# One raw weight piece requested ahead from step 16 on, and the rows' scatter released behind a finish: windowed attention with a mixture of experts on one core

## The chip, the cores and the metric

The kernel runs on one core of a Trainium2 chip, in one launch. The metric is the device time of an execution in microseconds. In what follows PE is TensorE, DVE is VectorE, ACT is ScalarE, POOL is GpSimd and SP is SyncE, which here only issues transfers.

## The reference

Attention over 8 batches of 8 heads, 576 positions, head width 64, with a causal window of 64. Its rows (4608 tokens of 512 values) go through a mixture of eight experts, each token through its best expert alone.

```python
scores = scale * np.matmul(q, k.transpose(0, 1, 3, 2))
mask = (rel >= 0) & (rel < window)                 # rel = i - j, window = 64
scores = np.where(mask, scores, -1000000000.0)
...
out_attn = np.matmul(attn, v)                      # softmax of scores, times v
x = out_attn.transpose(0, 2, 1, 3).reshape(B * S, H * D)
...
logits = x @ w_gate + modality_bias[modality_id]   # (4608, 8)
e_idx = np.argmax(logits, axis=1)
...
for e in range(E):
    h = np.maximum(x[mask] @ w1[e], 0.0)           # 512 -> 1024
    out[mask] = gate_w[mask, None] * (h @ w2[e])   # 1024 -> 512
```

## The kernel before

**Steps.** The attention is cut into 36 pairs of 64-row blocks, one pair of 128 tokens a step. The loop over `s` is a software pipeline written out by hand: in step `s` the scores of pair `s` are computed, the probabilities of pair `s-1` are turned, the values and the attention rows `xa` of pair `s-2` are made, and the router's logits of pair `s-3`. Every engine's order is the order in which the code is written (`manual_schedule`), so a line that is moved in the loop moves on each engine past whatever was recorded between its old and its new place.

**Rows.** Two pairs form a group G. `route1` to `route3` rank its tokens by expert; `rows` then turns the ranks into indices (L821, DVE) and POOL scatters the two pairs' rows into the scratch `xs` in DRAM, ordered by expert (L808 and L809). From group 4 on `rows` is not run at once but put into `held`; `release` runs what is left in `routing` (L752 to L765 on DVE) and then the held `rows`, once in each even step from 14 on. There are five `xa` buffers, so the attention rows of pair p+5 are written (L707) where those of pair p have been scattered from.

**Slots.** From step 12 on expert work is laid into the same loop. A slot is up to 256 rows of one expert, read back from `xs` into `xt`; `slot_pieces` is a generator that emits a slot's matmuls in 16 pieces, and `gap` takes the next piece. Steps from 12 on have four gaps each, so a slot spans four steps. What a piece leaves for other engines to do is put into `later`, and `run_later` emits it. `finish` is one such thing: it multiplies a half slot's result (`y0` or `y1`, 128x512 in PSUM) by the gate into an SBUF tile `y` (L334, DVE), and POOL scatters that tile to the output (L337). The first half's last matmuls are the first gap of steps 16, 20, 24, 28, 32 and 36, the second half's the fourth gap of the same steps; the second finish therefore stands on DVE just ahead of the next step's logits (L730) and attention rows (L707).

**Weights.** The weights of two experts are kept in SBUF, 16 pieces of 128x512 f32 each. A raw piece is loaded by SP (L103 or L107) into a tile `y`; a later call of `weights` rounds it into `Whi` (`split_hi`, L114, ACT), the call after that puts the rest into `Wlo` (`split_lo`, L119, DVE). Calls stand at the end of every step from 5 on, three a step in steps 12 to 15, and from step 16 on also in the middle of odd steps. The pieces 1 to 20 are requested by the end of step 15, the last at the end of step 23 or 24.

**The shared buffers.** Raw pieces and finished tiles both come from one pool, `y` with `bufs=4`. A new tile takes the buffer whose last use was emitted longest ago, and the writer waits until that use is over: for a finished tile until its scatter has landed.

Of the kernel before, what the change touches and what calls it, by code (L numbers as in the profile page):

```python
# [26 lines left out]
def tile_window_attn_moe(  # L27
# [39 lines left out]
    FIRST = 12  # L67
# [31 lines left out]
    def load_piece(raw, ev, c):  # L99

        if c * WCH < WC:
            ch, f0 = divmod(c * WCH, F)
            nc.sync.dma_start(  # L103
                out=raw, in_=w1_v[bass.ds(ev, 1), :, ch, f0:f0 + WCH].rearrange("o p f -> (o p) f"))
        else:
            c2 = c - WC // WCH
            nc.sync.dma_start(out=raw, in_=w2_v[bass.ds(ev, 1), :, c2, :].rearrange("o p f -> (o p) f"))  # L107
        return raw

    def split_hi(raw, buf, c):  # L110

        if Whi[buf] is None:
            Whi[buf] = wpool.tile([P, 2 * WC], F32R, name="Whi1")
        nc.scalar.copy(out=Whi[buf][:, c * WCH:(c + 1) * WCH], in_=raw)  # L114

    def split_lo(raw, buf, c):

        cols = slice(c * WCH, (c + 1) * WCH)
        nc.vector.tensor_tensor(  # L119
            out=Wlo[buf][:, cols], in0=raw, in1=Whi[buf][:, cols].bitcast(F32), op=ALU.subtract)  # L120
# [8 lines left out]
    def tick(n=1, table=False):  # L129
        for _ in range(n):  # L130
            if routing and not table:
                routing.pop(0)()
            elif queue:
                queue.pop(0)()
                issued[0] += 1
# [111 lines left out]
    def run_later():  # L247
        while later:
            later.pop(0)()
# [265 lines left out]
    def turn_bank(s):  # L515

        i = n_tp[0]
        n_tp[0] += 1
        if s < FIRST and i % 5 > 1:
            return ps_m.tile([P, 512], F32, name=("em", "y0", "y1")[i % 5 - 2])  # L520
        return ps_t.tile([P, 512], F32, name="tp")
# [31 lines left out]
    def quartered(G):  # L553

        return G >= QUARTERS and GBLK * G // BPB == (GBLK * G + GBLK - 1) // BPB
# [9 lines left out]
    def turn_heads(G, nm, i):  # L565

        dst = by_group(qT if nm == "q" else kT)[:, G % 2, 2 * i:2 * i + 2]
        nc.vector.transpose(
            out=dst.rearrange("p h j i -> p (h j i)"),
            in_=by_heads(qk[G, nm]).rearrange("p h u d -> p (h u d)"))  # L570
# [23 lines left out]
    def heads_t(G, nm, i, tp):  # L594


        src = plain(qk[G, nm], HP if quartered(G) else H).rearrange("p t (h a) d -> p t h (a d)", a=2)
        for h in range(2):
            for t in range(2):
                n = 2 * h + t  # L600
                turn(tp[:, n * P:(n + 1) * P], src[:, t, 2 * i + h])

    def heads_out(tp, G, nm, i, copy):
        dst = by_group(qT if nm == "q" else kT)[:, G % 2, 2 * i:2 * i + 2]
        copy(out=dst.rearrange("p h j (i t) -> p h t (j i)", t=2),
             in_=tp.rearrange("p (h t i) -> p h t i", h=2, t=2))
# [130 lines left out]
    def release():  # L737

        if held:
            tick(len(routing))  # L740
            held.pop(0)()
# [28 lines left out]
    def route2(G, tp):  # L770

        while routing:
            routing.pop(0)()
        oh = chosen[G]
        rk = tp[:, 0:GB * E]
        nc.tensor.matmul(
            out=rk, lhsT=tri, rhs=oh[:, 1:].rearrange("p j e -> p (j e)"), start=True, stop=False)
        for j in range(GB):
            sh = [P, GB - j, E]
            nc.tensor.matmul(  # L780
                out=rk[:, j * E:], lhsT=ones, rhs=oh[:, j:j + 1, :].broadcast_to(sh),
                start=False, stop=(j == GB - 1))
        return rk
# [117 lines left out]
    pieces = []  # L901
    raws = []
# [144 lines left out]
    def weights(s):  # L1047

        if halves:
            split_lo(*halves.pop(0))  # L1050
        if len(raws) == 2 or raws and not pieces:
            split_hi(*raws[0])
            halves.append(raws.pop(0))
        while pieces and len(raws) < 2:
            x, c = pieces.pop(0)
            raw = epool.tile([P, WCH], F32, name="y", bufs=4)
            raws.append((load_piece(raw, evs[x], c), x, c))

    for s in range(NPR + 4):
        j = s % GB  # L1060
        if s <= FIRST:
            for f, args in at.pop(s, ()):
                f(*args)
        n_tick = 6 if s < FIRST else 5
        n_gap = 0 if s < FIRST else 4
        G = s // GB + 1
        heads = PARTS[j] if G < NG else ()
        R = (s - 5) // GB if s >= 5 and j == 1 else -1

        def part(i):  # L1070
            if not heads:
                return
            if i == 1 and quartered(G):
                turn_heads(G, *heads[1])
                return
            tp = turn_bank(s)
            heads_t(G, *heads[i], tp)
            heads_out(tp, G, *heads[i], nc.scalar.copy if heads[i] == K1 else nc.vector.tensor_copy)

        def ranks():  # L1080
            if R < 0:
                return None
            tp = turn_bank(s)
            rk = route2(R, tp)
            n = None
            if R == NG - 1 or any(R == T for T, _ in EARLY):
                n = counts_out(tab if R == NG - 1 else pl, counts(R, tp))
            route3(R, rk)
            return n
        if 1 <= s < FIRST:  # L1090
            swap_upper(s - 1)

        if 2 <= s < NPR + 2:
            values(s - 2)
            if s <= FIRST:
                values_out(s - 2)
        if 3 <= s < NPR + 3:
            logits(s - 3, turn_bank(s) if s != FIRST else ps_m.tile([P, 512], F32, name="y0"))
            if (s - 3) % GB == GB - 1:
                route1((s - 3) // GB)  # L1100
        if FIRST < s < NPR + 2:
            values_out(s - 2)
        if s < NPR:
            scores(s)
            if s == FIRST:
                x_turn(fetched[0])
                gap(it, True)
            minima(s)
            if s == FIRST - 2:
                tick(todo[0][-1] - issued[0], table=True)  # L1110
        if 1 <= s <= NPR:
            if s == FIRST:
                run_later()
            if s >= FIRST:
                swap_upper(s - 1)
            swap_v(s - 1)
            for a in range(2):
                probs_t(s - 1, a, turn_bank(s))
            sums(s - 1)
        if s < NPR:  # L1120
            exps(s, (0, 1))
        if s == 0:
            first_pair(1, (both[:1], both[1:]))
            cast_bias()
        if s <= FIRST:
            if s >= 2:
                x_t(s - 2, turn_bank(s) if s != FIRST else ps_m.tile([P, 512], F32, name="y0"))
            run_later()
            tick(2)
            if s < NPR:  # L1130
                exps(s, (2, 3, 4))
            part(0)
            if s == FIRST:
                weights(s)
                gap(it, True)
            run_later()
            tick(n_tick)
            cnt = ranks()
            exps(s, (5, 6, 7))
        else:  # L1140
            release()
            gap(it, True)
            run_later()
            tick(2)
            if s < NPR:
                exps(s, (2, 3, 4))
            if s < FIRST + 4 or s % 2:
                weights(s)
            for f, args in at.pop(s, ()):
                f(*args)  # L1150
            gap(it, True)
            cnt = ranks()
            if s < NPR + 2:
                x_t(s - 2, turn_bank(s))
            part(0)
            run_later()
            tick(n_tick)
            if s < NPR:
                exps(s, (5, 6, 7))
        if n_gap > 2:  # L1160
            if FIRST <= s < FIRST + 4:
                weights(s)
            gap(it, True)
        part(1)
        run_later()
        tick(n_tick)
        if s == WEIGHTS:
            load_weights()
        if s >= WEIGHTS:
            weights(s)  # L1170
        if n_gap > 3:
            gap(it, True)
        run_later()
        if s == 1:
            select_bias()
        if s == 4:
            nc.sync.dma_start(out=xs_blk[DUMMY:DUMMY + 2].rearrange("b p c -> p b c"), in_=padrow)
        for T, xs_ in EARLY:
            if T == R:
                plan(T, xs_, cnt)  # L1180
# [271 lines left out]
```

## Time and profile before

| what | value |
|---|---|
| median of 3 runs | 629.34 us (627.99 to 630.23) |
| the profiled execution, its own time | 624.07 us |
| span of the profiled execution, first to last instruction | 622.3 us |
| granted TensorE clock, mean | 0.989 of full speed |
| PE busy | 600.2 us (96%) |
| DVE, ACT, POOL busy | 389.3, 293.7, 140.9 us |

Steps 12 to 35 of the attention loop lie between 75.84 and about 330 us, most of them 10.0 to 10.8 us long; behind them only slots are worked off. In a row of instructions in order of time the first number is the start, the second the length, both in us; then engine, line, operation, what it writes and reads, shapes, and in brackets how long the engine was idle before and what ended that. A row of the waits has the total, the number of times and the longest. In a table by stretch each engine has its busy time; PEclk is the granted clock.

### The profile page before, as it was taken

The page shows a single profiled execution, that of the slowest core. Times are in us where ns is not written, and L with a number is a line of the kernel's source. Part 1 is how long each engine was busy: PE and PEld are TensorE (multiplying, and loading weights), DVE is VectorE, ACT ScalarE, POOL GpSimd, SP SyncE. Part 2 cuts the span into 40 slices and gives each one's busy share as a digit, 9 for nine tenths or more (in the row PEclk, how much of TensorE's full clock was granted, in tenths as well). Part 3 has the DMA queues.
Part 4 walks back from the last instruction along what each step waited for, and adds up shares of the span by engine and source line. Part 5 has one row for each costly group of instructions (what it writes and reads, how often), then busy time and mean ns, then how long its engine had stood idle before and what let it go on. Part 6 is the DMA issues. An engine that isn't in the chain of part 4 may idle for free.

```text
span 622.3 us, 17338 instructions
## 1 busy us (share of the span) xinstructions
PE 600.2 (96%) x6309; PEld 537.6 (86%) x6309; DVE 389.3 (63%) x1493; ACT 293.7 (47%) x926; POOL 140.9 (23%) x315
## 2 busy tenths in 40 slices
PE   7999889979999989999999999999999999999996
PEld 5888778868889878988898899899999999989986
DVE  3899988857867776767656365323224734776621
ACT  3899885753756556555553111111112513554411
POOL 6333322132142212320423131011001111102202
PEclk7999999999999999999999999999999999999999
DMA  9998957656757735554513034622243534678300
GB/s 167 219 242 213 223 159 181 158 152 152 171 152 183 197 84 137 154 111 102 148 53 105 35 101 151 188 71 69 44 159 101 171 135 136 190 252 241 114 17 22
DMA packets 175111, 88.08 MB, mean 142 GB/s; under 512 B 138746, under 2 KB 157744, under 8 KB 174896
## 3 DMA queue, kind: packets, MB, share of 16 engines
q1 hardware_dynamic: 166400, 67.46, 44.6%
q0 software_dynamic: 5888, 18.93, 8.1%
q8 instruction: 50, 0.82, 0.5%
q10 hardware_dynamic: 2736, 0.58, 0.5%
q14 instruction: 37, 0.30, 0.2%
HBM read 67.49 MB, written 23.91 MB: 147 GB/s over the span
## 4 chain that ended last, share of the span: by engine, by line
PE 70%; DVE 5%; DMA 5%; SPq 3%; issue 2%; ACT 2%; POOL 1%; POOLq 0%; DVEq 0%; ACTq 0%
PE y L326 27%; PE em L304 19%; PE sp L304 10%; PE tp L470 6%; PE av L696 2%; PE sp L640 2%; DMA out_dram<-y,id 2%; SPq L590 2%; DMA xs_scratch<-xa,idx 1%; PE tp L725 1%; DVE xt L266 1%; PE y L377 1%; DMA xt<-xs_scratch 1%; DVE xl L196 1%; POOL xs_scratch L809 1%
## 5 line engine op out<-in xcount | busy, mean ns | idle before, releaser
L326 PE MATMUL y<-Whi,hh 128*128 128x512 f32 x288 | 116.3, 404 | 0.0
L666 ACT ACTIVATE ss<-ss,mn 128x128 f32<-128x128 f32 x288 | 112.2, 397 | 6.6 <-DVE mn L654 6.6
L326 PE MATMUL y<-Wlo,hh 128*128 128x512 f32 x288 | 113.2, 393 | 0.0
L326 PE MATMUL y<-Whi,hl 128*128 128x512 f32 x288 | 112.9, 392 | 0.0
L313 DVE SCALAR_TENSOR_TENSOR hl<-em,hh 128x512 fp32r<-128x512 f32 x50 | 34.4, 689 | 79.5 <-ACT hh L312 79.1
L337 POOL DMA_INDIRECT out_dram<-y,id x36 | 39.7, 1104 | 191.0 <-DVE y L334 160.8
L304 PE MATMUL em<-xh,Whi 128*128 128x256 f32 x400 | 81.7, 285 | 0.0
L304 PE MATMUL em<-xl,Whi 128*128 128x256 f32 x400 | 79.2, 279 | 0.0
L304 PE MATMUL em<-xh,Wlo 128*128 128x256 f32 x400 | 79.1, 279 | 0.0
L312 ACT ACTIVATE hh<-em 128x512 fp32r<-128x512 f32 x50 | 29.9, 599 | 100.5 <-PE em L304 95.5
L675 ACT COPY pT<-tp 128x512 f32<-128x512 f32 x57 | 31.5, 589 | 83.3 <-PE tp L470 83.0
L809 POOL DMA_INDIRECT xs_scratch<-xa,idx x36 | 36.6, 1017 | 128.9 <-DVE e_n_p L154 58.9
L326 PEld LDWEIGHTS y<-Whi,hl 128*128 128x128 f32 x288 | 54.3, 189 | 12.2
L654 DVE CUSTOM_DVE_ANT_0 ss<-sp,masks 128x128 f32<-128x128 f32 x288 | 63.4, 285 | 2.3 <-PE sp L640 2.3
L304 PEld LDWEIGHTS em<-xh,Whi 128*128 128x128 f32 x400 | 62.8, 188 | 2.3
L326 PEld LDWEIGHTS y<-Whi,hh 128*128 128x128 f32 x288 | 54.7, 190 | 8.9
L326 PEld LDWEIGHTS y<-Wlo,hh 128*128 128x128 f32 x288 | 54.5, 189 | 8.5
L304 PEld LDWEIGHTS em<-xh,Wlo 128*128 128x128 f32 x400 | 60.9, 188 | 0.0
L304 PEld LDWEIGHTS em<-xl,Whi 128*128 128x128 f32 x400 | 60.8, 188 | 0.0
L666 ACT ACTIVATION_READ_ACCUMULATOR ss<-ss,mn 128x1 f32 x288 | 55.9, 194 | 0.0
L312 ACT ACTIVATE hh<-sp 128x512 fp32r<-128x512 f32 x22 | 13.1, 597 | 76.1 <-PE sp L304 76.1
L696 PEld LDWEIGHTS av<-ve,pT 128*64 128x64 f32 x576 | 36.3, 138 | 12.6 <-issue 8.1
(242 smaller groups left out, 1201.7 us busy)
## 6 DMA issues: line engine op xcount, KB each, us to landing
xt<-xs_scratch SPq DMA_DIRECT2D x72, 128.0 KB, 2.9
vo<-in_v_dram SPq DMA_DIRECT2D x32, 256.0 KB, 3.3
y<-in_moe_w_dram SPq DMA_DIRECT2D x32, 256.0 KB, 2.8
vo<-in_moe_w_dram SPq DMA_DIRECT2D x24, 256.0 KB, 3.6
ss<-in_moe_w_dram SPq DMA_DIRECT2D x24, 256.0 KB, 4.2
xs_scratch<-xs_scratch SPq DMA_DIRECT2D x8, 514.0 KB, 5.8
pT<-in_moe_w_dram SPq DMA_DIRECT2D x16, 256.0 KB, 4.5
qk<-in_k_dram SPq DMA_DIRECT2D x22, 128.0 KB, 3.9
```

What stands on the lines that cost most here:

```text
L304: nc.tensor.matmul(out=hb[:, i * TP:(i + 1) * TP], lhsT=w[buf][:, c0:c0 + P], rhs=x[:, c * TP:(c + 1) * TP], start=(n == 0), stop=(n == le ...
L312: nc.scalar.activation(out=hh, in_=hb, func=AF.Relu),
L313: nc.vector.scalar_tensor_tensor(out=hl, in0=hb, scalar=0.0, in1=hh.bitcast(F32), op0=ALU.max, op1=ALU.subtract)))
L326: nc.tensor.matmul(out=sl["y", t], lhsT=h[:, i * TP + t * P:i * TP + (t + 1) * P], rhs=w[buf][:, c0:c0 + DM], start=(k == 0 and n == 0), s ...
L337: ins = nc.gpsimd.indirect_dma_start(out=out, out_offset=bass.IndirectOffsetOnAxis(ap=sl["id"][:, t:t + 1], axis=0), in_=y, in_offset=None ...
L470: nc.tensor.transpose(out=out_, in_=in_, identity=ident[p0:p0 + n, p0:p0 + n])
L590: dma.dma_start(out=by_heads(t)[rows, (h - nh) // 2, u, :], in_=src.rearrange("(u p) d -> p u d", p=R32))
L654: nc.vector.tensor_tensor_reduce(out=ss[a][:, hp, :], in0=sp[a][:, hp * P:(hp + 1) * P], in1=mask, scale=-1.0 / 8.0, scalar=3.0e38, op0=AL ...
L666: nc.scalar.activation(out=ss[a][:, hp, :], in_=ss[a][:, hp, :], func=AF.Exp, bias=mn[:, h:h + 1], scale=-1.0, accum_out=sm[:, h:h + 1])
L675: nc.scalar.copy(out=pT, in_=pp)
L696: nc.tensor.matmul(out=by_block(av)[c * W64:(c + 1) * W64, a, :, hp, :], lhsT=pT[:, i:i + W64], rhs=(vo if c else ve)[p][:, 2 * hp + a, :] ...
L809: ins = nc.gpsimd.indirect_dma_start(out=xs, out_offset=bass.IndirectOffsetOnAxis(ap=idx[:, j:j + 1], axis=0), in_=xg[j], in_offset=None)
```

## The change

Two edits in the loop of steps. From step 16 on `weights` keeps one raw piece requested ahead instead of two: `n` is 1, so the call at the end of step 16 requests nothing, and each later call first converts the one piece at hand and then requests the next. And in steps from 13 on `release` stands behind the first gap and its `run_later` instead of ahead of them.

```diff
         if halves:
             split_lo(*halves.pop(0))
-        if len(raws) == 2 or raws and not pieces:
+        n = 2 if s < FIRST + 4 else 1
+        if len(raws) >= n or raws and not pieces:
             split_hi(*raws[0])
             halves.append(raws.pop(0))
-        while pieces and len(raws) < 2:
+        while pieces and len(raws) < n:
             x, c = pieces.pop(0)
             raw = epool.tile([P, WCH], F32, name="y", bufs=4)
             raws.append((load_piece(raw, evs[x], c), x, c))
...
         else:
-            release()
             gap(it, True)
             run_later()
+            release()
             tick(2)
```

The order of PE and ACT stays as it was. On DVE and POOL it changes in six places, steps 16, 20, 24, 28, 32 and 36, all alike; on SP the loads of the raw pieces 21 to 32 move.

DVE in step 16, ahead of the change: the copy of `ve`, the routing operations that `release` runs (`lm` to `oh`), the indices of the rows (`idx`) and the first finish (`y` from `y_2120`, the slot's `y0`).

```order
L543 COPY ve<-vo 64x512
L752 TENSOR_REDUCE lm<-lg 128x2
L753 TENSOR_TENSOR lg<-lg,lm 128x16
L757 SCALAR_TENSOR_TENSOR wn<-lg,desc 128x16
L759 TENSOR_REDUCE wm<-wn 128x2
L760 TENSOR_TENSOR oh<-wn,wm 128x16
L765 TENSOR_REDUCE oh<-oh 128x8
L821 CAST idx<-dst 128x2
L334 TENSOR_SCALAR y<-y_2120,gate 128x512
L605 COPY kT<-tp 128x2x2x128
```

The same place with the change:

```order
L543 COPY ve<-vo 64x512
L334 TENSOR_SCALAR y<-y_2120,gate 128x512
L752 TENSOR_REDUCE lm<-lg 128x2
L753 TENSOR_TENSOR lg<-lg,lm 128x16
L757 SCALAR_TENSOR_TENSOR wn<-lg,desc 128x16
L759 TENSOR_REDUCE wm<-wn 128x2
L760 TENSOR_TENSOR oh<-wn,wm 128x16
L765 TENSOR_REDUCE oh<-oh 128x8
L821 CAST idx<-dst 128x2
L605 COPY kT<-tp 128x2x2x128
```

The finish moved ahead of the seven routing operations, and these behind it.

POOL in the same step, before: the two row scatters (`xs_scratch`) and the scatters of the two finished tiles, `y_2659` of the first half and `y_2737` of the second.

```order
L808 COPY xa0_101<-idc_210 128x1
L809 DMA xs_scratch<-xa0_101,idx_2496 39168x514
L808 COPY xa1_102<-idc_210 128x1
L809 DMA xs_scratch<-xa1_102,idx_2496 39168x514
L336 MEMSET pause_100 1x1
L337 DMA out_0_dram<-y_2659,id_1854 4608x512
L337 DMA out_0_dram<-y_2737,id_1854 4608x512
```

With the change, where the two finished tiles are called `y_2647` and `y_2735`:

```order
L336 MEMSET pause_100 1x1
L337 DMA out_0_dram<-y_2647,id_1854 4608x512
L808 COPY xa0_101<-idc_210 128x1
L809 DMA xs_scratch<-xa0_101,idx_2496 39168x514
L808 COPY xa1_102<-idc_210 128x1
L809 DMA xs_scratch<-xa1_102,idx_2496 39168x514
L337 DMA out_0_dram<-y_2735,id_1854 4608x512
```

The first half's scatter moved ahead of both row scatters and their small copies; the second half's stays behind them. (A second `pause` ahead of the last row is left out in both.)

SP at the turn from step 16 to 17, before, with the raw pieces 21 and 22 (`y_2729`, `y_2843`) and 23 (`y_2918`):

```order
L590 DMA qk_2670<-in_q_dram 32x8x32 x8
L107 DMA y_2729<-in_moe_w2_dram 128x512
L107 DMA y_2843<-in_moe_w2_dram 128x512
L529 DMA vo_2845<-in_v_dram 128x8x64
L584 DMA qk_2847<-in_k_dram 128x4x64 x2
L590 DMA qk_2847<-in_k_dram 32x8x32 x8
L103 DMA y_2918<-in_moe_w1_dram 128x512
```

With the change (`y_2841` is piece 21, `y_2916` piece 22; address computations between the loads are left out in both):

```order
L590 DMA qk_2670<-in_q_dram 32x8x32 x8
L107 DMA y_2841<-in_moe_w2_dram 128x512
L529 DMA vo_2843<-in_v_dram 128x8x64
L584 DMA qk_2845<-in_k_dram 128x4x64 x2
L590 DMA qk_2845<-in_k_dram 32x8x32 x8
L107 DMA y_2916<-in_moe_w2_dram 128x512
```

One raw load fewer stands ahead of step 17's loads of `v` and `k`; from there on each place in the queue carries the piece that stood one place earlier.

The four `y` buffers, A to D by address, as the two built programs hand them out from step 16 on (first finish, second finish, and the raw piece requested next):

| step of the first finish | before | with the change |
|---|---|---|
| 16 | C, C, then raw in C | C, C, then raw in B |
| 20 | A, D, with a raw in A between them and one in D behind | C, C, with a raw in A between them and one in D behind |
| 24 | B, B | C, C, with a raw in B between them |
| 28 | C, B | A, C |
| 32 | A, D | D, B |
| 36 | C, B | A, C |

## The prediction

> **What bounds the kernel now.** I read the page first, then busy time by stretch, the waits, and the instructions in order of time around the longest wait. The page says that TensorE is nearly always busy and carries most of the chain that ended last:
>
> ```profile
> PE 600.2 (96%) x6309; PEld 537.6 (86%) x6309; DVE 389.3 (63%) x1493; ACT 293.7 (47%) x926; POOL 140.9 (23%) x315
> PE 70%; DVE 5%; DMA 5%; SPq 3%; issue 2%; ACT 2%; POOL 1%; POOLq 0%; DVEq 0%; ACTq 0%
> ```
>
> So an edit off TensorE counts only where TensorE stands still. A table by step finds such places. These rows are steps 17, 21, 25, 29 and 33, each from its first score matmul to that of the next step; the columns are length, busy time by engine, granted clock, DMA share, GB/s.
>
> ```profile
> core 0: us, PE busy (x) PEld busy (x) DVE busy (x) ACT busy (x) POOL busy (x), PEclk, DMA share, GB/s
> 127.89:143.90 16.01, 12.30 (x141) 10.44 (x137) 7.73 (x34) 6.35 (x22) 3.76 (x8) 0.89 0.53 134
> 174.77:185.46 10.69, 10.69 (x144) 9.52 (x141) 7.72 (x34) 6.24 (x22) 3.20 (x6) 1.00 0.62 166
> 216.20:229.12 12.92, 10.99 (x144) 9.50 (x140) 7.80 (x34) 5.85 (x21) 2.88 (x6) 1.00 0.48 120
> 259.93:270.72 10.79, 10.79 (x143) 9.52 (x140) 6.05 (x31) 5.23 (x20) 2.87 (x6) 1.00 0.58 139
> 301.11:311.26 10.15, 10.15 (x140) 9.12 (x136) 6.01 (x30) 5.23 (x20) 2.87 (x6) 1.00 0.49 133
> ```
>
> Steps 21, 29 and 33 are as long as TensorE is busy. Steps 17 and 25 are not: 3.71 and 1.93 us idle, and in step 17 the granted clock falls to 0.89 as well. The waits of VectorE and of the SP queue name what was late:
>
> ```profile
> DVE y L334 <- DMA out_dram<-y,id: 8.1, 2, 5.1
> DVE xa L707 <- DMA xs_scratch<-xa,idx: 0.5, 1, 0.5
> SPq L107 <- DMA out_dram<-y,id: 18.5, 3, 10.4
> ```
>
> Two waits of VectorE, 8.1 us in all, are for an output scatter that must land before its `y` buffer is written again. Here is the longer one, VectorE first, then POOL, then what followed on ACT and PE:
>
> ```profile
> 122.31 0.17 DVE L752 TENSOR_REDUCE lm<-lg 128x2 f32<-128x16 f32 x1
> 123.51 0.75 DVE L334 TENSOR_SCALAR y<-y,gate 128x512 f32<-128x512 f32 x1
> 126.86 0.68 DVE L119 TENSOR_TENSOR Wlo<-y,Whi 128x512 fp32r<-128x512 f32 x1
> 132.68 0.75 DVE L334 TENSOR_SCALAR y<-y,gate 128x512 f32<-128x512 f32 x1 [5.14 <-DMA out_dram<-y,id]
> 133.69 0.69 DVE L707 TENSOR_TENSOR xa<-av,rw 128x512 f32<-128x512 f32 x1
> ...
> 124.39 1.05 POOL L809 DMA_INDIRECT xs_scratch<-xa,idx  x1 [5.74 <-DVE y L334]
> 125.92 0.96 POOL L809 DMA_INDIRECT xs_scratch<-xa,idx  x1 [0.28 <-POOL xa L808]
> 127.19 1.22 POOL L337 DMA_INDIRECT out_dram<-y,id  x1 [0.22 <-DVE hl L313]
> 133.71 0.99 POOL L337 DMA_INDIRECT out_dram<-y,id  x1 [5.25 <-DVE rw L704]
> ...
> 134.69 0.40 ACT L666 ACTIVATE ss<-ss,mn 128x128 f32<-128x128 f32 x1 [3.04 <-DVE mn L654]
> 137.50 1.08 PE L470 MATMUL tp<-ident_r,qk 128*128 128x128 f32 x4 [2.40 <-issue]
> ```
>
> `y0` (the first finish, 123.51) is ready at 124.26, yet POOL issues its scatter at 127.19, behind both scatters of the rows. `y1` (the second finish) takes the same buffer; VectorE was free for it at 127.54 and waits until 132.68. The minima come late, ACT's exponentials behind them, and TensorE waits for a bank.
>
> **The change, part by part.** *The rows' release behind the finish* takes POOL's two row scatters (some 2.8 us, 124.39 to 127.19) and VectorE's seven small routing operations (122.31 to 123.51) from in front of `y0` in steps 16, 20, 24, 28, 32 and 36. In step 16 `y0` then starts at 122.31 and takes 0.75; `y1`'s scatter shows 0.28 from the end of the write (133.43) to the issue (133.71), so `y0`'s issues at 122.31 + 0.75 + 0.28 = 123.34 instead of 127.19. POOL was idle there (5.74). When does it land? The chain gives 5.36 for the old place behind the rows and, for a second row scatter, 4.11; the view of line 337 gives minimum, median and maximum of all output scatters:
>
> ```profile
> 127.19 5.36 DMA out_dram<-y,id
> 150.93 4.11 DMA xs_scratch<-xa,idx
> ...
> DMA to landing us min/median/max: 2.7/4.1/6.8
> ```
>
> So it lands at 126.0, 127.4 or 130.1 against the 127.54 at which `y1` wants the buffer: a wait of 0, 0 or 2.6. The median is the nearest value, since the scatter is alone in front of its queue but beside loads of `q`: no wait. The Trainium skill ("DMA: Bandwidth & Descriptors", section on the anatomy of one DMA, SWDGE path) gives about 2.0 us plus bytes over 436 GB/s for a DMA from GpSimd, an estimate of 2.6 us for this 256 KB; by that it would land at 125.9 and the sum would be the same. The row's minimum is near it, its median is not, so the row is used.
>
> Steps 20/21 and 24/25 go by these rows:
>
> ```profile
> 168.76 0.17 DVE L752 TENSOR_REDUCE lm<-lg 128x2 f32<-128x16 f32 x1
> 174.58 0.75 DVE L334 TENSOR_SCALAR y<-y,gate 128x512 f32<-128x512 f32 x1
> 175.60 0.69 DVE L707 TENSOR_TENSOR xa<-av,rw 128x512 f32<-128x512 f32 x1
> 170.83 1.05 POOL L809 DMA_INDIRECT xs_scratch<-xa,idx  x1 [7.43 <-DVE y L334]
> ...
> 210.18 0.17 DVE L752 TENSOR_REDUCE lm<-lg 128x2 f32<-128x16 f32 x1
> 218.94 0.75 DVE L334 TENSOR_SCALAR y<-y,gate 128x512 f32<-128x512 f32 x1 [2.99 <-DMA out_dram<-y,id]
> ```
>
> In step 24 the same working gives an issue at 211.21 and a median landing at 215.3, before the 215.95 at which VectorE is free: this wait goes too. In step 20 the new allocation makes `y0` and `y1` share a buffer where they did not: issue 169.79, median landing 173.9, needed at 174.58: no wait; with 6.8, 2.0 us.
>
> What the two stalls are worth. Step 17: against step 33, whose `q` heads are turned in the same way, 16.01 − 10.15 = 5.9; by its own row 3.71 idle plus 0.11 × 16.01 = 1.8 of lost clock, 5.5. I take 5.6. Step 25: against the mean of 21 and 29 (10.74) 2.2, by idle 1.9; I take 2.1. Together 7.7, with ends 7.4 and 8.1. Step 25 also shows how much lateness of VectorE is hidden: a wait of 2.99 lengthened the step by 2.18, so 0.8 costs nothing.
>
> The rows pay for it. Their indices come 0.66 later (one `y` write), and the first row scatter moves from 124.39 to about 125.05 (POOL is through with `y0`'s at 124.56 and still copies ids for 0.2). The five `xa` buffers go round, so L707 of the next step waits for just this scatter. All row scatters, minimum, median, maximum:
>
> ```profile
> DMA to landing us min/median/max: 3.1/4.2/6.1
> ```
>
> In step 17 it lands at 128.2, 129.3 or 131.2; without the stall L707 would start 1.01 after `y1`, at 128.55: a wait of 0, 0.7 or 2.6, of which 0.8 is hidden. In step 21 (171.49 + 4.2 = 175.7 against 175.60) it is 0.1. I take nothing, with 1.8 as the end for step 17. In step 36 `y0` now reaches VectorE before its matmuls end:
>
> ```profile
> 332.88 0.17 DVE L752 TENSOR_REDUCE lm<-lg 128x2 f32<-128x16 f32 x1
> 333.20 0.40 PE L326 MATMUL y<-Whi,hl 128*128 128x512 f32 x1
> ```
>
> That is 333.60 − 332.88 = 0.7 us, under the 0.8.
>
> *One raw piece ahead* moves twelve loads (pieces 21 to 32) one call of `weights` later and past the `vo`, `q`, `k` or slot loads of that call on SP; the conversions stay. It also frees SP: the raw load of step 17 gets a buffer that VectorE's subtraction frees, not `y1`'s, so SP's waits for output scatters (18.5 us) mostly go. By itself I give that nothing: step 21 stands behind the 10.4 us wait and is no longer than step 29, which has none. The price is a shorter lead. Shortest is step 19, where the load follows a slot's load:
>
> ```profile
> y<-in_moe_w_dram SPq DMA_DIRECT2D x32, 256.0 KB, 2.8
> ...
> 158.38 0.36 SPq L103 DMA_DIRECT2D y<-in_moe_w_dram  x1
> 161.62 0.61 ACT L114 CAST Whi<-y 128x512 fp32r<-128x512 f32 x1
> 162.56 1.14 ACT L195 CAST xh<-xt 128x512 fp32r<-128x512 f32 x2 [0.32 <-DVE xt L266]
> 165.79 1.26 ACT L675 COPY pT<-tp 128x512 f32<-128x512 f32 x2 [2.10 <-PE tp L470]
> ```
>
> The piece now converted at 161.62 is the one issued at 158.38: 3.24 us for a landing of 2.8. Should it come a microsecond late, 0.32 of it falls into ACT's idle time, the slot's cast (162.56) moves by 0.7, and ACT has caught up before its next copy, which waits 2.10 for TensorE: under the 0.8, so 0 to 0.2 on TensorE. I put 0.2 for all new waits together.
>
> Sum: −5.6 − 2.1 + 0.2 = −7.5 us, from 624.07 to about 616.6 in the profiled execution (span 622.3 to 614.8). The median of the runs, 629.34, lies 5.3 above that execution and nothing in the trace says where; I carry it over unchanged: **621.8 us**. About 0.3%, 1.9 us, is what a measurement of this kernel can tell from no change.
>
> **The rivals.** *Only part of the stall goes:* `y0`'s scatter, now next to SP's unblocked loads, lands as late as the slowest row. With 6.8 us the waits at steps 17, 21 and 25 are 2.6, 2.0 and 2.1, less 0.8 hidden each, 4.3 in all: 626.1. With the 5.36 of the old place only 0.4 is left at step 17: 622.2. For it: both share the 16 DMA engines, 48% to 62% busy in the table by step. Against: 5.36 was measured behind two row scatters.
>
> *It does not do what it says:* both finishes still share one buffer in steps 16/17 and 24/25, now in 20/21 too. If the landing hung on traffic and not on the time of issue, `y1` would wait as long as before: about 629. Against it: issued at 123.34, `y0`'s scatter would need 9.2 us to land at 127.19 + 5.36 = 132.55 as before, and the slowest took 6.8.
>
> *Slower:* the rows become the late transfer. L707 waits for them in steps 17, 21, 25, 29 and 33. It decides once each of the five costs (7.5 + 1.9) / 5 = 1.9 us, that is a wait of 2.7; in step 21 a landing 6.8 us after the issue. At 7.2, and with the other steps like 21, each costs 2.3, 11.5 in all: 633.3. The second row scatter of a pair, itself behind another, landed in 4.11, and the longest of all took 6.1, which speaks against. The Trainium skill (same page, section on queues, rings and completion order) says that each DMA engine takes descriptors in ring order, which would put the rows behind the output; the 4.11 shows little of it.
>
> **How the numbers follow.** Both stalls go, 621.8: 0.74. Part of it, 622.2 to 626.1: 0.13. No effect: 0.08. Slower: 0.05. The first two are faster: 0.87; 0.08 same; 0.05 slower. The likeliest alone spans 619.9 (8.1 saved, from the lowest run shown, 627.99) to 623.0 (7.4 saved less the 0.2, from the highest, 630.23). The range reaches on into the partial case: 619.8 to 625.5.
>
> **What would show it.** Right: step 17 at 10.2 to 10.8 with clock 1.00, step 25 near 10.8, no wait of `y` L334 for `out_dram` over 1 us, SP's L107 waits for `out_dram` gone. Wrong: L334 waits in step 21, L707 waits for `xs_scratch` over 1 us, or ACT L114 waits for a raw piece and TensorE with it.

## The result, and the profile after

The changed kernel took **618.69 us** (median of 4 runs, 618.52 to 619.48); the kernel before, with one more run beside it, 628.66 us (626.99 to 630.23). The ratio is 0.984, 95% interval 0.982 to 0.987: 10.0 us faster, 1.6%. The forecast was 621.8 with a range down to 619.8: the direction was right, the gain a third larger than forecast, the time 1.1 us below the range. Between the two *profiled* executions the gain is smaller: 624.07 to 618.77 us, 5.3. That these two differences disagree is what the experiments had to explain.

First the changed kernel's page, its busy times and its chain:

```profile
PE 596.8 (97%) x6309; PEld 534.2 (87%) x6309; DVE 389.0 (63%) x1493; ACT 292.7 (47%) x926; POOL 139.2 (23%) x315
PE 77%; DVE 5%; ACT 2%; issue 1%; DMA 1%; SPq 0%; POOL 0%; POOLq 0%; DVEq 0%; ACTq 0%
```

DMA had 5% of the chain and SP's queue 3%; they have 1% and nothing. The table by step, columns as in the prediction, for steps 16, 17, 21, 24, 25 and 33:

```profile
core 0: us, PE busy (x) PEld busy (x) DVE busy (x) ACT busy (x) POOL busy (x), PEclk, DMA share, GB/s
116.78:127.87 11.09, 10.49 (x137) 9.15 (x133) 9.41 (x37) 5.94 (x22) 4.41 (x9) 1.00 0.72 180
127.87:139.60 11.73, 10.44 (x140) 9.10 (x137) 7.80 (x34) 6.35 (x22) 2.86 (x6) 1.00 0.79 184
170.70:181.43 10.73, 10.73 (x145) 9.55 (x141) 7.70 (x34) 6.15 (x22) 2.86 (x6) 1.00 0.70 166
201.65:212.59 10.94, 10.74 (x141) 9.48 (x137) 8.88 (x43) 6.33 (x23) 3.49 (x6) 1.00 0.72 185
212.59:223.31 10.72, 10.72 (x144) 9.55 (x140) 7.77 (x34) 5.63 (x21) 2.86 (x6) 1.00 0.54 128
295.30:305.45 10.15, 10.15 (x139) 9.13 (x136) 6.03 (x30) 5.23 (x20) 2.87 (x6) 1.00 0.46 118
```

Step 25 is down from 12.92 to 10.72, all of it PE. Step 17 is down from 16.01 to 11.73 at full clock, but 1.3 us of PE's idle time is left. Steps 16 and 24 have grown by 0.4 (from 10.68 and 10.52). Three rows of PE show where: the two probability turns of step 17 in the profile before and in the changed kernel's, then the last logits of the changed kernel's step 16.

```profile
130.31 0.66 PE L470 MATMUL tp<-ident_r,ss 128*128 128x128 f32 x4 [0.73 <-ACT pT L675]
...
130.85 0.66 PE L470 MATMUL tp<-ident_r,ss 128*128 128x128 f32 x4 [1.29 <-ACT pT L675]
...
127.58 0.36 PE L725 MATMUL tp<-wg,xaT 128*64 128x8 f32 x6 [0.16 <-issue]
```

What is left in step 17 is a wait for ACT's copy of the probabilities (`pT`), which the profile before already has, at 0.73. The growth of step 16 lies in its last matmuls, the logits, around a gap that nothing in the profile ends ("issue"). The finishes and scatters of steps 16 and 17, DVE first, then POOL:

```profile
127.70 0.74 DVE L334 TENSOR_SCALAR y<-y,gate 128x512 f32<-128x512 f32 x1
122.93 1.05 POOL L337 DMA_INDIRECT out_dram<-y,id  x1 [5.10 <-DVE lg L753]
124.75 0.98 POOL L809 DMA_INDIRECT xs_scratch<-xa,idx  x1 [0.55 <-POOL xa L808]
126.20 0.98 POOL L809 DMA_INDIRECT xs_scratch<-xa,idx  x1 [0.28 <-issue]
128.72 0.98 POOL L337 DMA_INDIRECT out_dram<-y,id  x1 [1.46 <-DVE lg L730]
```

`y0`'s scatter issues at 122.93 (forecast 123.34, before 127.19), the rows' first at 124.75 (forecast 125.05), and `y1` starts at 127.70 with no wait in its row. This step 16 began 0.43 earlier than the one forecast from; counted from its start, `y0`'s scatter issues when forecast and the rows' 0.1 later. Two waits of the changed kernel are worth a look (total, times, longest):

```profile
ACT ex L756 <- DVE lg L753: 14.8, 14, 2.8
DVE xa L707 <- DMA xs_scratch<-xa,idx: 1.0, 2, 0.8
```

and the one of them that was shorter in the kernel before:

```profile
ACT ex L756 <- DVE lg L753: 10.1, 14, 2.8
```

The rows' scatters cost L707 next to nothing: the 0.8 is in step 7, which the change does not touch, and from step 16 on there is one wait of 0.2, in step 33. The other wait has grown: ACT's exponential of the router (`ex`) waits 4.7 us longer in all for `lg`, which now stands behind `y0` on DVE. ACT works in order, so what is behind `ex`, the copy of `xaT`, is late, and PE stands 0.2 us for it in each of steps 20 and 24, though not in step 16.

### The profile page after: what moved, and what is told of

Same layout as the page of the kernel before. It is cut to its first block, busy times and chain, and to the rows that moved or that the text cites. A ratio compares the mean times of both kernels' runs of the same rounds, so it can differ in the third digit from the quotient of the medians.

```text
span 617.0 us, 17344 instructions
## 1 busy us (share of the span) xinstructions
PE 596.8 (97%) x6309; PEld 534.2 (87%) x6309; DVE 389.0 (63%) x1493; ACT 292.7 (47%) x926; POOL 139.2 (23%) x315
## 4 chain that ended last, share of the span: by engine, by line
PE 77%; DVE 5%; ACT 2%; issue 1%; DMA 1%; SPq 0%; POOL 0%; POOLq 0%; DVEq 0%; ACTq 0%
PE y L326 29%; PE em L304 21%; PE sp L304 10%; PE tp L470 7%; PE av L696 3%; PE sp L640 3%; PE tp L725 1%; DVE xt L266 1%; PE y L377 1%; DVE ss L654 1%; ACT ss L666 1%; DVE xl L196 1%; DMA xs_scratch<-xa,idx 1%; PE sp L352 0%; PE em L352 0%
```

## The experiments

Two theories at the start. *Theory 1:* the gain is the stall of steps 17 and 25, where `y1` waits for `y0`'s scatter; edit 2 carries it, and ordinary executions of the kernel before have a longer one than the profiled execution. *Rival:* edit 1, which frees SP and deals the buffers out differently, carries a good part. The times, each against the kernel before run beside it on the same chip (626.1 to 626.4 us there, on chips 13 and 4; which chip the result above comes from is not on record):

| kernel | median us | ratio to before (95%) |
|---|---|---|
| before, again | 626.55 | 1.000 (0.998 to 1.002) |
| edit 1 alone | 627.19 | 1.002 (1.000 to 1.004) |
| edit 2 alone | 618.33 | 0.988 (0.986 to 0.991) |
| changed kernel, all routing ahead of the finish | 620.89 | 0.992 (0.989 to 0.994) |
| changed kernel, again | 619.37 | 0.989 (0.987 to 0.991) |
| changed kernel, two routing operations ahead | 617.73 | 0.986 (0.984 to 0.989) |
| the same on edit 2 alone | 619.05 | 0.987 (0.985 to 0.990) |
| the same on the changed kernel, up to step 24 only | 617.06 | 0.985 (0.983 to 0.988) |
| before, pause ahead of the third scatter, steps 28 and 32 | 624.74 | 0.998 (0.996 to 0.999) |
| before, pause ahead of the fourth scatter, same steps | 622.75 | 0.995 (0.993 to 0.997) |

And the lengths of the steps that matter, from the tables by step of each profile, first score matmul to first score matmul:

| step | before, 1st profile | before, 2nd | before, 3rd | edit 1 | edit 2 | changed, 1st | changed, 2nd | all routing first | two first, up to 24 |
|---|---|---|---|---|---|---|---|---|---|
| 16 | 10.68 | 11.57 | 11.56 | 11.75 | 11.04 | 11.09 | 11.05 | 10.68 | 11.09 |
| 17 | 16.01 | 12.79 | 15.15 | 12.97 | 11.15 | 11.73 | 11.77 | 11.09 | 11.11 |
| 20 + 21 | 21.45 | 21.99 | 22.00 | 23.58 | 21.75 | 21.76 | 21.82 | 21.59 | 21.30 |
| 24 + 25 | 23.44 | 23.90 | 24.02 | 23.53 | 21.96 | 21.66 | 21.70 | 22.55 | 21.25 |
| 28 + 29 | 21.23 | 22.77 | 22.23 | 22.66 | 21.22 | 21.23 | 21.23 | 22.64 | 21.23 |
| 32 + 33 | 20.17 | 21.87 | 21.71 | 21.82 | 20.16 | 20.17 | 20.17 | 21.82 | 20.16 |

**The kernel before once more.** No edit; a second profile and more times.

> The kernel before, unchanged, for another profile and five more times. Theory 1 (the whole gain is the two stalls, and they are longer in ordinary executions of before than in the profiled one of 624.1 us): times of 627 to 630 us, and in this profile step 17 or step 25 is longer than 16.0 and 12.9 us, by about 3 to 5 us in all, with longer waits of y L334 for out_dram or a second half-clock window behind them. Rival 2 (before's ordinary executions lose the 5 us elsewhere, at the start, at the end or in many small gaps that the change removes too): steps 17 and 25 as in the first profile and the extra time in other rows.

Measured: 626.55 us. Step 17 is *shorter* than in the first profile, 12.79 against 16.01: the wait is there, at 4.4 us instead of 5.1, but no half-speed clock. Of the 3.2 us, 1.5 are PE's idle time and 1.7 its busy time (12.30 to 10.59). The time is in the steps that the first profile had shown clean. Steps 17, 28, 29, 32 and 33 of this second profile:

```profile
128.71:141.50 12.79, 10.59 (x137) 9.13 (x136) 7.96 (x34) 6.35 (x22) 3.19 (x6) 1.00 0.55 136
248.02:259.28 11.26, 10.82 (x141) 9.69 (x137) 8.27 (x41) 5.96 (x22) 4.12 (x7) 1.00 0.58 155
259.28:270.79 11.51, 11.34 (x142) 9.75 (x141) 5.97 (x31) 5.23 (x20) 2.10 (x6) 1.00 0.46 105
291.13:301.51 10.38, 10.18 (x136) 9.04 (x133) 8.82 (x41) 5.43 (x21) 3.71 (x7) 1.00 0.54 134
301.51:313.00 11.49, 10.96 (x137) 9.47 (x136) 5.93 (x30) 5.23 (x20) 2.54 (x6) 1.00 0.44 112
```

The last four take 44.64 us against 41.40 in the first profile, at full clock, and no buffer is shared there. The same profile in order of time at the turn to step 33, PE (logits L725, scores L640), then POOL:

```profile
300.63 0.58 PE L725 MATMUL tp<-wg,xaT 128*64 128x8 f32 x15
301.41 0.17 PE L725 MATMUL tp<-wg,xaT 128*64 128x8 f32 x1 [0.20 <-issue]
301.51 0.43 PE L640 MATMUL sp<-kT,qT 64*64 64x128 f32 x3
302.17 0.44 PE L640 MATMUL sp<-kT,qT 64*64 64x128 f32 x3 [0.23 <-issue]
302.91 0.85 PE L640 MATMUL sp<-kT,qT 64*64 64x128 f32 x21 [0.30 <-issue]
...
297.04 1.05 POOL L809 DMA_INDIRECT xs_scratch<-xa,idx  x1 [7.81 <-DVE e_n_p L154]
298.61 0.96 POOL L809 DMA_INDIRECT xs_scratch<-xa,idx  x1 [0.28 <-POOL xa L808]
299.87 1.00 POOL L337 DMA_INDIRECT out_dram<-y,id  x1 [0.21 <-issue]
301.18 0.99 POOL L337 DMA_INDIRECT out_dram<-y,id  x1 [0.25 <-issue]
```

PE dribbles, as I call it from here on: three matmuls, a gap, three more, with "issue" in the brackets, that is, nothing in the profile that it waits for. The 32 score matmuls, which take 1.10 us in step 33 of the first profile, stretch over 2.25. It sets in as POOL issues its fourth scatter in a row. So the rival of this expectation holds: before's ordinary executions also lose time elsewhere, and Theory 1 names only part of the gain.

**Each edit alone.** Edit 1 keeps `release` ahead of the gap; edit 2 keeps two raw pieces ahead.

```diff
 (edit 1 alone)
         else:
+            release()
             gap(it, True)
             run_later()
-            release()
 (edit 2 alone)
-        n = 2 if s < FIRST + 4 else 1
-        if len(raws) >= n or raws and not pieces:
+        if len(raws) == 2 or raws and not pieces:
```

> Edit 1 alone: one piece of raw weights requested ahead from step 16 on, the rows released ahead of the finish as before. y0's scatter still issues behind the rows' two. In the built program y0 and y1 of steps 16/17 get different buffers, those of 20/21 the same one. Theory 1 (the issue of y0's scatter behind the rows is what stalls, the buffer only decides where): step 17 about 11 us, and step 21 or 25 stalls instead by some 2 to 6 us, so 619 to 627 us. Rival 2 (edit 1 is what frees SP and removes the stalls by itself): 617 to 619 us, as low as the changed kernel. A stall that stays where it was would give 627 to 630 us.

> Edit 2 alone: the rows released behind the first finish, two raw pieces ahead as before. Theory 1 (early issue of y0's scatter carries the gain): 618 to 620 us, no wait of y L334 for out_dram over 1 us; SP's waits for out_dram may stay and cost nothing. Rival 2 (edit 1 carries it): about 624 to 629 us.

Edit 2 alone has the whole gain, edit 1 alone none (627.19). From the waits of edit 1 alone, and its steps 17 and 21:

```profile
DVE y L334 <- DMA out_dram<-y,id: 6.1, 2, 3.1
```

```profile
128.35:141.32 12.97, 12.44 (x138) 10.76 (x136) 7.42 (x33) 6.30 (x22) 2.65 (x6) 0.87 0.72 169
172.41:184.98 12.57, 11.07 (x141) 9.57 (x141) 7.81 (x34) 6.37 (x22) 2.88 (x6) 1.00 0.76 188
```

With edit 1 the two finishes of step 16 no longer share a buffer, those of step 20 do: the stall moves from step 17 to step 21 (12.57 against 10.69), as Theory 1 said. The buffer decides where the stall is, the late issue that there is one. Step 17 stays long all the same, from the dribble and a stretch of half clock (PEclk 0.87), though no finish waits in it. From SP's waits in edit 2 alone:

```profile
SPq L107 <- DMA out_dram<-y,id: 10.6, 2, 5.7
```

SP still stands 10.6 us for output scatters there, and it costs nothing, as the prediction assumed.

**All routing ahead of the finish.** The changed kernel with only the rows behind it.

```diff
         else:
+            if held:
+                tick(len(routing))
             gap(it, True)
```

> The changed kernel, with the seven small routing operations put back ahead of the finish's y0, and only the rows' copies and scatters behind it. In the built program the two probability turns of step 17 then get different PSUM banks (the same one in the changed kernel). Theory 1: routing ahead of y0 costs y0's scatter about 1.0 us of lead, still early enough; ACT's ex no longer waits in steps 16, 20, 24, so each is 0.3 to 0.4 us shorter, and step 17 up to 1.3 us shorter by the other bank: 616 to 618 us. Rival 2 (the lead of y0's scatter is already used up): y L334 waits for out_dram again, 1 us or more in step 17, and the time is 619 us or above.

Neither: `y1` does not wait, step 16 is back at 10.68, and yet the time is 620.89. Counted from the start of their step, the rows' scatters issue 0.9 us later in steps 28 and 32, and the dribble is back. The rows are also late for L707, which waits 1.7 us for them in step 17 (not at all there in the changed kernel). Its steps 29 and 33, and POOL's last two scatters of step 32:

```profile
253.28:265.35 12.07, 11.56 (x142) 9.90 (x140) 5.97 (x31) 5.24 (x20) 2.79 (x6) 1.00 0.47 114
296.29:307.54 11.25, 10.84 (x137) 9.36 (x135) 5.93 (x30) 5.25 (x20) 2.58 (x6) 1.00 0.43 115
```

```profile
294.71 0.98 POOL L809 DMA_INDIRECT xs_scratch<-xa,idx  x1 [0.28 <-issue]
296.00 0.99 POOL L337 DMA_INDIRECT out_dram<-y,id  x1 [0.21 <-issue]
```

The order of the scatters is the changed kernel's, their distance is not: these two, the second of the rows and `y1`'s, issue 1.29 us apart, 1.93 in the changed kernel's step 32. Steps 28, 29, 32 and 33 take 44.46 us, as in before's second profile. So a second theory: *the dribble comes when POOL's scatters follow one another without a pause at the turn of the step, and edit 2 removes it by pulling `y0`'s scatter out of the row.*

**Taking the row of scatters apart in the kernel before.** Eight more 1x1 memsets on POOL (1.26 us for nine) ahead of the third scatter, `y0`'s, or ahead of the fourth, `y1`'s, in steps 28 and 32 alone, where no buffer is shared. Nothing else changes.

```diff
-            nc.gpsimd.memset(pause, 0.0)
+            n0 = st["n0"] = st.get("n0", 0) + (t == 0); [nc.gpsimd.memset(pause, 0.0) for _ in range(9 if t == 0 and n0 in (4, 5) else 1)]
```

(`t == 1` for the fourth.)

> The kernel before, with eight more 1x1 memsets on POOL ahead of the first finish's scatter in steps 28 and 32 alone, so that it issues 1 to 2 us behind the second row scatter instead of 0.3. In the second profile of before steps 28, 29, 32 and 33 took 44.6 us together with PE gaps that nothing in the profile ends, 41.4 in the first profile. Theory (PE is held up while three scatters that follow each other closely are worked off): the gaps go or shrink, 41.4 to 43 us. Rival (they come from something else in those steps): 44 to 45 us as before. If this execution is like the first profile of before, steps 20 and 24 also show 10.8 and 10.5 us and it tells nothing.

> The kernel before, with the eight extra memsets ahead of the second finish's scatter in steps 28 and 32, so that the fourth scatter issues about 1 us later and the third where it did. If it is the third scatter behind the rows' two that holds PE up: steps 28, 29, 32 and 33 stay at 44 to 45 us together. If it is the fourth, issued while PE runs its short matmuls: 42 to 43.5 us, as with the pause ahead of the third (42.9).

Ahead of the third: 42.87 us for the four steps, 1.7 us less in the times; step 29 keeps 11.87, its gaps now behind the score matmuls. Ahead of the fourth: 41.71, as good as clean, and 3.4 us less (1.7 to 4.3 by the interval of the ratio). Steps 16 and 24 of the same two executions, where nothing was paused, still dribble, so it is not that these executions happened to be clean. The kernel before is made faster by idling POOL for 1.2 us in two places. Steps 29 and 33 with the pause ahead of the fourth, then the turn to step 33 on POOL and PE:

```profile
258.95:269.78 10.83, 10.83 (x143) 9.54 (x140) 6.03 (x31) 5.33 (x20) 3.24 (x9) 1.00 0.57 137
300.34:310.52 10.18, 10.18 (x135) 9.15 (x135) 5.93 (x30) 5.23 (x20) 3.56 (x12) 1.00 0.51 133
```

```profile
298.87 1.00 POOL L337 DMA_INDIRECT out_dram<-y,id  x1 [0.22 <-issue]
299.83 1.26 POOL L336 MEMSET pause<- 1x1 f32 x9
301.82 1.00 POOL L337 DMA_INDIRECT out_dram<-y,id  x1 [0.73 <-DVE xa L707]
299.64 0.59 PE L725 MATMUL tp<-wg,xaT 128*64 128x8 f32 x16
300.34 1.17 PE L640 MATMUL sp<-kT,qT 64*64 64x128 f32 x32
```

Three scatters in a row are still there, the fourth issues 2.95 us behind the third instead of 1.31, and the 32 score matmuls run through. My expectation, that either the third or the fourth alone is to blame, was too simple: moving either helps, moving the fourth more.

**The kernel before, a third profile.**

> The kernel before once more, for a third profile. If PE's gaps in steps 16, 20, 24, 28 and 32 belong to ordinary executions on this chip: step lengths within 0.3 us of the second profile's, so 44.3 to 45.0 us for steps 28, 29, 32 and 33 together, and a time of 624 to 629 us. If they come and go from one execution to the next: 41.4 us for these four, as in the first profile.

It took 627.84 us; the four steps took 43.94, and steps 17 and 33 read

```profile
128.39:143.54 15.15, 12.13 (x137) 10.27 (x136) 7.93 (x34) 6.36 (x22) 3.20 (x6) 0.89 0.56 126
303.28:314.56 11.28, 10.81 (x137) 9.36 (x136) 5.94 (x30) 5.23 (x20) 2.48 (x6) 1.00 0.42 113
```

So before has two extras: the half-clock stretch in step 17 (PEclk 0.89) and the dribble. The first profile had the former only (624.07), the second the latter only (626.25), the third both (627.84). The half-clock stretch comes and goes. The dribble is missing in the first profile alone; all five later ones with before's order on POOL (edit 1 alone and the two pauses among them) have it in steps 16 and 24. Whether it differs from execution to execution, or between the first series and the later ones, these profiles do not tell. The four steps are 0.4 under the expected 44.3, since step 28 was clean.

**The changed kernel again, and less of the routing behind the finish.** The last three runs put `lm` and `lg`, on which ACT's `ex` waits, back ahead of the finish.

```diff
         else:
+            if held:
+                tick(2)
             gap(it, True)
```

(In the last of the three `if held and s < FIRST + 16`, that is up to step 24.)

> The changed kernel, unchanged, beside edit 2 alone (618.33 us, 7.8 below its before). If edit 1 adds nothing: 618 to 619 us on the same chip, 7 to 8 us below before. If edit 1 helps once edit 2 is there: 617 us or less. In the profile steps 28, 29, 32 and 33 at 10.4, 10.8, 10.0 and 10.2 us with no gap of PE ended by nothing that the profile shows, as in its first profile.

> The changed kernel with the first two routing operations (lm and lg, 0.34 us of DVE) back ahead of the finish, the rest behind it. Theory: ACT's ex gets lg in time, so steps 16, 20 and 24 lose the 0.3 to 0.4 us that they gained; y0's scatter issues 0.3 us later, the rows when they did; the two probability turns of step 17 get different PSUM banks, worth 0.5 us. 616.5 to 618 us. Rival: the start of the scatters against PE's stretch of short matmuls is what counts, and 0.3 us later brings PE's gaps back as in the run with all routing first: 619 to 621 us.

> The same two operations put first, on edit 2 alone (two raw pieces ahead). Theory: 0.5 to 1.5 us under edit 2 alone, 617 to 618 us, with no y L334 wait for out_dram over 1 us. Rival: as for the run before, 619 to 621 us.

> The run with two routing operations first (617.73 us beside a before of 626.41), but only in steps up to 24; steps 28, 32 and 36 as in the changed kernel. Theory: step 33 goes back from 10.90 to 10.15 us and the gain in steps 17, 20 and 24 stays: 616.5 to 617.5 us, 9 us or more under before. Rival (the longer step 33 there was chance): as that run, 617.3 to 618.3 us.

The changed kernel repeats its steps (table above) and is 7.0 us under before on this chip; edit 1 adds nothing that can be told. With two operations first, ACT's wait is back at 10.1 us, and the two probability turns of step 17 no longer write the same PSUM bank in the built program: step 17 takes 10.24, for the first time what step 33 takes. But in step 32 `y1`'s scatter issues a quarter of a microsecond earlier against PE, the dribble is back in step 33, and there the expected gain is given away. Step 16 did not shrink either (11.20), and step 20 hardly (10.96). Steps 17 and 33 of that run:

```profile
128.20:138.44 10.24, 10.24 (x138) 9.12 (x136) 7.70 (x34) 6.26 (x22) 2.87 (x6) 1.00 0.73 154
293.74:304.64 10.90, 10.60 (x138) 9.37 (x136) 5.93 (x30) 5.24 (x20) 2.67 (x6) 1.00 0.43 112
```

Restricted to the steps up to 24, step 33 is clean; steps 17, 20, 24 and 33 of the last run:

```profile
127.85:138.96 11.11, 10.55 (x139) 9.10 (x136) 7.73 (x34) 6.46 (x22) 2.86 (x6) 1.00 0.72 160
159.04:169.64 10.60, 10.60 (x141) 9.47 (x137) 8.41 (x35) 6.37 (x23) 3.49 (x6) 1.00 0.57 164
200.56:211.10 10.54, 10.54 (x141) 9.48 (x137) 9.20 (x43) 6.33 (x23) 3.50 (x6) 1.00 0.78 210
293.79:303.94 10.15, 10.15 (x139) 9.13 (x135) 5.93 (x30) 5.23 (x20) 2.87 (x6) 1.00 0.47 119
```

617.06 us, 9.1 under before and the best median of all, by 2.3 us under the changed kernel's second series (two series on two chips, the kernel before 0.2 apart in them). From the run with two operations first in every step, 617.73, it is not told apart: the intervals of the two ratios overlap. Its step 17 shows how thin the margin is: `y0`'s scatter issues 0.3 us later and this time lands late, so that `y1` starts 5.7 us behind that issue; 4.8 were enough in the changed kernel.

```profile
128.96 0.75 DVE L334 TENSOR_SCALAR y<-y,gate 128x512 f32<-128x512 f32 x1 [1.80 <-DMA out_dram<-y,id]
```

On edit 2 alone the same two operations bring nothing (619.05): there step 17 keeps both turns in one bank (11.33), step 33 dribbles (10.87), and the profiled execution, 620.56 us, also has a granted clock of 0.85 in step 12.

## Why the prediction was wrong in size, point by point

- **The stalls (5.6 and 2.1).** Shown right in kind: no wait of `y` for `out_dram` over 1 us is left, step 25 is 10.72 (forecast near 10.8), SP's L107 waits are gone, step 21 does not stall. Step 25 gave 2.2. Step 17 gave 4.28 and stands at 11.73, not at the forecast 10.2 to 10.8: I took step 33 as its floor and counted all of its 3.71 us of idle time to the stall. But 0.73 of that was PE's wait for ACT's copy between the two probability turns, which share a PSUM bank; the change leaves this wait, and it measured 1.29 in the changed kernel (0.73 with edit 2 alone; why it grew is open). Where the turns got two banks, in the runs with all routing and with two operations first, it is gone, and the latter reached 10.24. The 2.40 us of idle time that I called a wait for a bank has "issue" in its row: the profile names nothing that ended it.
- **Routing behind `y0` (costed at nothing).** Mis-sized. I counted the seven operations as time that `y0` gains and did not ask who waits for them: ACT's `ex`. Steps 16, 20 and 24 grew by 0.41, 0.27 and 0.42, 1.1 us together, against 0.2 for all new waits. In steps 20 and 24 this is the late `xaT`: with `lm` and `lg` ahead, up to step 24, they are back at 10.60 and 10.54. Step 16 is not (11.09); its 0.4 is the gap in the logits, a remnant of the dribble in the changed kernel, and not the routing.
- **Rows' scatter later, raw piece's lead shorter (0 to 0.2).** Right: from step 16 on L707 waits at most 0.2 in the changed kernel's first profile and 0.6 in its second, and ACT's conversions (L114) wait for no raw piece there.
- **The sum in the profiled executions.** −4.28 − 2.20 + 1.1 is −5.4, measured −5.3; the forecast was −7.5. The two errors above, the wait in step 17 and the growth of steps 16, 20 and 24, made it too large.
- **"I carry it over unchanged".** This is the step that failed and decided the outcome. The 5.3 us between the profiled execution and the median were not a constant. The changed kernel's median (618.69) equals its profiled execution (618.77), so what before's ordinary executions had on top is gone too. In the later series such a surplus is seen: the dribble, 2.5 to 3.2 us in steps 28, 29, 32 and 33 (43.94 and 44.64 against 41.40), and 2.1 in steps 16, 20 and 24, of which the changed kernel's growth there takes 1.1 back. Edit 2 removes it in steps 28 to 33, and the pauses do there, in part or almost wholly. Like with like, the second profiles of before and of the changed kernel differ by 7.1 us in the steps of the table: 1.0 in step 17, 2.2 in 24 and 25, 3.2 in 28, 29, 32 and 33, 0.7 in 16, 20 and 21; the medians there by 7.0. Before's dribble adds up to 4.6 to 5.4 us: that the 5.3 of the first series were the same dribble fits, but is not shown, since no profile of an ordinary execution was taken there.
- **What was luck.** That the forecast missed the range by only 1.1 us. The gain of the profiled execution was put 2.2 us too large, what came on top of it, 4.7 of the 10.0, at nothing.
- **The rivals.** None of the three happened in the changed kernel; the first, a `y0` scatter that lands late, did in the last run (1.80 in step 17). The fourth case, more gain than the one stall explains, was not on the list, since I read the clean steps 28 to 33 of one execution as clean in all.

**What stays open.** What holds PE up while scatters are issued in a row. The first profile of before has the same order and nearly the same distances (its fourth scatter issued at 301.11, as step 33 began) and no gaps, so the distance is not the whole condition. Whether it is POOL's issuing or the transfers themselves was not separated. A late transfer of instructions does not explain it everywhere: around the dribble at the turn to step 29 of the second profile (257.9 to 261.2 us) the queues that the profile calls "instruction" move nothing. Open, too, is why before is 2.5 us slower in the first series than in the others.

## What to carry to other kernels

If the profiled execution lies outside the runs' range, the difference is part of the problem: take a second profile before carrying it over, because a change may remove it. When a piece of work is moved behind another, list the readers of each operation in it, on every engine that works in order, not only of the last one. And scatters that POOL issues directly behind one another can go with lost TensorE time, as here, even where nobody waits for their data: a pause between them can be the cheaper order.

## What the runs showed of the hardware that was not expected

- PE can be held up with no wait in the profile: groups of three matmuls 0.7 us apart, 32 score matmuls in 2.25 instead of 1.10 us, around the time when POOL issues its third or fourth indirect scatter in a row. Idling POOL for 1.2 us in two places gave back 3.4 us.
- The same stall can come with or without a fall of the granted clock: step 17 of the same program took 12.79 us at full clock and 16.01 or 15.15 with a granted clock of 0.89, in each of which 3.4 us ran at half clock behind 2.4 or 2.3 us in which PE stood. What sets it off is open: edit 1 alone had 3.4 us at half clock in step 17 with no gap of PE above 0.5 us there or in the step before.
